# Output pass with seven products in seven of eight token blocks, and all of x turned by TensorE, in place of the second half of x transposed by DMA

## The chip, the cores and the metric

The program runs on one core of one Trainium2 chip. The metric is the device time of one execution in microseconds (us), the median over several runs. Times inside an execution come from the hardware profiler, and are counted from the first instruction. The engines are TensorE (PE; its loads of stationary operands are PEld), VectorE (DVE), ScalarE (ACT), GpSimd (POOL) and SyncE (SP). SP and POOL issue most of the DMA transfers, each from a queue that it works through in order.

## The reference

A gate mixes a spectral filter with a two-layer perceptron, and the program computes the output and eight gradients:

```python
g = sigmoid((x * gate_w).sum(-1, keepdims=True))
a = irfft2(rfft2(x) * (w_r + 1j * w_i))          # spectral filter over (S, D)
h = relu(B_x @ w1 + b1) ** 2                     # inside the vjp as below
b = h @ w2 + b2
out = g * a + (1 - g) * b
# outputs: out, and the gradients of x, w_r, w_i, w1, b1, w2, b2, gate_w for grad_out
```

In the reference the perceptron reads the same `x` as the filter. Here S = 2048 tokens, D = 1024, F = 3584, and inputs and outputs are bf16. In the program, "x" is that input and "grad" is `grad_out`.

## The kernel before, in words

Tokens are cut into 16 tiles of 128 rows, numbered 0 to 15. TensorE carries three large stages one after the other, and the spectral filter is a side generator (`aside`) whose steps `spread` puts between them at a set rate.

**`mlp_in` (0 to about 475 us).** It makes the hidden layer and its gradient, transposed. Its first 32 steps ("units", numbered `u` from 0) work on the first four column blocks of w1 and w2: eight `forth` units (product `ph`, 8 matmuls of 128x512, then on ACT `rT` (relu) and `h2T` (square)), eight `back_` units (product `pd`, 8 matmuls, then one DVE operation into `dhT`) for tokens 0 to 1023; then the same sixteen for tokens 1024 to 2047. A `forth` unit needs four tiles of `xT` (x turned, features on the partitions), a `back_` unit four tiles of `dbT` (the gradient turned). Products take their PSUM banks from a ring of two.

Each tile of x is loaded by SP (`rows_of_x`, tile `xsrc`, eight buffers). `turn_tile` turns a tile: eight 128x128 transposes on TensorE into a PSUM buffer `pt` (a ring of two, tag `tr`), then one copy out of it. Copies into `xT` are mostly ACT's, copies into `dbT` are DVE's. `weigh(i)` is a DVE operation that reads `xsrc` and leaves the gate's sum for the tile (`gsum`). `gate(i0)` takes four such sums, runs two sigmoids on ACT (`omg`, `gcol`) and then four DVE operations that scale the gradient tiles (`dbn`).

In this kernel, x tiles 0 to 7 are turned by TensorE, and tiles 8 to 15 reach `xT` by DMA transposes that SP issues (`turned`), four ahead of the loads of tiles 8 to 11 and four ahead of tiles 12 to 15. `weigh` for a tile after the third is ordered behind the last copy out of a `pt` buffer (`later["copied"]`), and so are `gate`'s scalings. `gate(4)` stands behind unit 6, `gate(8)` behind 15, `gate(12)` behind 19. After unit 17 the first-stage loads (`xs`, tile `src`) and the first `folds` of the filter are put in; `folds` starts with two DVE operations into `uv` and goes on with small ACT copies into `f` (line 263 is the first of them).

All engines execute in order. The order on each engine is fixed when the program is built: a scheduler places the instructions, and `after(..., NoSync)` adds ordering without a wait.

**`mlp_grads` (475 to 837 us).** The gradients of w2 and w1, with seven products in place of eight (sums and differences of quarter matrices, made by DVE).

**`mlp_out` (837 us to the end).** First the output rows. w2's left half (`cL`) is there already; its right half (`cR`, tile `w2R`) is loaded by seven SP transfers of 512 KB. Tokens come in eight blocks of 256 (`load("h", k)`, `even` and `odd` buffers in turn). Here the first two blocks (`N0 = 2`) are done plainly: for each token tile `t` and half `hf` of the columns, 28 matmuls of 128x512 into `acc`, in the order of `steps`. The other six blocks use `Block`, seven chains of 14 matmuls: `p1`, `p2`, `p6`, `p5`, `p7`, `p4`, `p3`. They need four sums of quarters of w2 (`w2_sums`, made by DVE in four steps, names `T1` to `T4`; T3 is written over `cR`) and four sums per block (`sums`, `S1` to `S4`, tiles `dS`). Chain `p6` reads S2 and T2, `p5` reads S1 and T1, `p7` S3 and T3, `p4` T4, `p3` S4. `prepare(t)` (ACT `na`, DVE `v`), `close(t)` (DVE `cu`, a reduction, ACT `scaled`) and `put(t)` finish a token tile. All DVE work of this stage is chained in program order by `dve`, all ACT work by `act`.

The filter's last part (`fft_out`) runs beside it until block 5. For each of its tiles TensorE does `pki` (8 small matmuls, from the ACT copies `re` and the DVE sums `rf`) and `pui` (8 small matmuls); ACT copies `rt` and `e`; DVE does `ev`, `tt`, `yo`. POOL loads `r` and stores `yo`.

Of the kernel before, what the change touches and what calls it, by code (L numbers as in the profile page):

```python
# [10 lines left out]
P = 128  # L11
# [3 lines left out]
ALU = mybir.AluOpType  # L15
# [125 lines left out]
def kernel(  # L141
# [89 lines left out]
    def of_tile(i):  # L231
        return slice(P * i, P * (i + 1))

    def after(ins, earlier, wait=mybir.DependencyClass.Sync):

        if earlier is not None:
            info = mybir.DependencyInfo(wait, mybir.DependencyReason.DATA)
            tc.add_manual_dep(ins.ins, earlier.ins.name, info, reason="paced")
# [375 lines left out]

    def rows_of_w2(t_, fc, half, tie=None):
        src = B_w2[fc * P : (fc + 4) * P, half * H : (half + 1) * H]
        after(ld(out=t_[:, fc : fc + 4, :], in_=src.rearrange("(q p) e -> p q e", p=P)), tie)

    db_p, db_s = pool("db")
    dbn = db_p.tile([P, NT, D], BF16, name="dbn", tag="dbn")  # L620
# [22 lines left out]
    def turn_tile(dst, i, src, copy, tie=None):  # L643

        pt = tps.tile([P, DC, P], BF16, name="pt", tag="tr", bufs=2)
        for b in range(DC):
            later["turned"] = nc.tensor.transpose(pt[:, b, :], src[:, b * P : (b + 1) * P], identb[:])
            after(later["turned"], tie, mybir.DependencyClass.NoSync)
        later["copied"] = copy(out=dst[:, :, of_tile(i)], in_=pt[:])

    def vectors(vrow):
        vps = tps.tile([P, FC], BF16, name="vps", tag="tr", bufs=2)
# [8 lines left out]
        nc.scalar.copy(out=gwb[:], in_=pb[:])  # L661
        return gwb

    def weigh(i, src, tie):
        unused = f1.tile([P, 2, H], FDT, name="uv", tag="uv", bufs=2)
        weighed = nc.vector.tensor_tensor_reduce(
            out=unused[:].rearrange("p a b -> p (a b)"), in0=src[:], in1=gwb[:], scale=1.0, scalar=0.0,
            op0=ALU.mult, op1=ALU.add, accum_out=gsum[:, i : i + 1],
        )
        after(weighed, tie, mybir.DependencyClass.NoSync)  # L670

    def gate(i0):

        c_ = slice(i0, i0 + 4)
        nc.scalar.activation(omg[:, c_], gsum[:, c_], ACT.Sigmoid, scale=-1.0)
        nc.scalar.activation(gcol[:, c_], gsum[:, c_], ACT.Sigmoid)
        for i in range(i0, i0 + 4):
            later["scaled"] = nc.vector.tensor_scalar(out=dbn[:, i, :], in0=dbn[:, i, :], scalar1=omg[:, i : i + 1], scalar2=None, op0=ALU.mult)
            after(later["scaled"], later["copied"], mybir.DependencyClass.NoSync)

    def first_stage_of_x():
        f, ft = {0: folds(f1, xs[0], later["last"])}, {}
# [160 lines left out]
    def mlp_grads():  # L843
# [151 lines left out]
        class Turned(Block):  # L995

            def operands(self):
                (self.a11, self.a12), (_, self.a22) = quads(xr, H)
                (self.b11, self.b21), (_, self.b22) = quads(grp[self.g], FH)
                self.S, self.T = X_, T_.setdefault(self.g, {})  # L1000

            flat = staticmethod(lambda ap: ap.rearrange("p (j f) -> p j f", j=2))

# [3 lines left out]
                return t_  # L1007

            def add(self, t_, h, kept):
                ins = super().add(t_, h, kept)  # L1010
                in_turn(ins, "DVE")
                turn["DVE"] = ins
                return ins

            def side(self, t_, h):
                return t_.rearrange("p (j h f) -> p h j f", j=2, h=2)[:, h]
# [39 lines left out]
        def sums_of_group(g, *which, tie=None):  # L1056
            (g11, g21), (g12, g22) = quads(grp[g], FH)
            made = T_.setdefault(g, {})
            for n in which:
                if n == 3:  # L1060
                    made[3] = fp16(g12)
                else:
                    tag = {1: "S3", 2: "S2", 4: "S4"}[n]
                    made[n] = sb.tile([P, KH, FH], FP16, name=f"G{n}", tag=tag, bufs=2 if n == 1 else 1)[:]
                x, y = {
                    1: lambda: (g12, g11),
                    2: lambda: (g22, made[1]),
                    3: lambda: (g22, g12),
                    4: lambda: (g21, made[2]),
                }[n]()  # L1070
                ins = V(out=made[n], in0=x, in1=y, op=ALU.subtract)
                after(ins, tie, mybir.DependencyClass.NoSync)
                if g > FG:
                    in_turn(ins, "DVE")
                    turn["DVE"] = ins

        NB = 2 * len(jobs)
        each, slow, none = 0.5, 0.25, 1e-6
        for k in range(2):
            blk[k] = Block(k)  # L1080
        fetch(1, 0, 1)
# [85 lines left out]
        fetch(FG + 1, 1)  # L1167
        yield each
        c.p1()
        yield slow  # L1170
        c.p2()
        yield slow
        sums_of_x(3, tie=c.first)
        b.p5()
        sums_of_group(FG, 4, 3)
        fetch(FG + 2, 0)
        yield slow
        b.p6()
        yield slow
        c.p5()  # L1180
        yield slow
        c.p6()
        sums_of_x(4)
        yield each
        b.p7()
        yield each
        c.p7()
        yield each
        b.p4()
        yield each  # L1190
# [3 lines left out]
        for k in range(NB // 2 + 2, NB):  # L1194
            g, second = divmod(k, 2)
            b = Turned(k)
            b.p1()
            if not second:
                sums_of_group(g, 1, 2)
            yield each  # L1200
            b.p2()
            if second:
                fetch(g + 2, 0)
            yield each
            a.p4()
            if not second:
                sums_of_group(g, 3, 4)
            yield each
            b.p6()
            yield each  # L1210
            a.p3()
            if not second:
                fetch(g + 1, 1)
            yield each
            b.p5()
            yield each
            b.p7()
            yield each
            n = k - NB // 2 - 2
            if n < FC // 4:  # L1220
                rows_of_w2(later["w2L"], 4 * n, 0, b.added)
            a = b
# [23 lines left out]
    def mlp_out():  # L1246
# [37 lines left out]

        def fetch_a(t):
            a_[t] = row("a_", FDT)
            ld(out=a_[t][:], in_=ax_scr[0][t][:])

        def fetch_g(t):
            go[t] = row("go3", BF16)  # L1290
            ld(out=go[t][:], in_=go_perm[t])

        def prepare(t):
            na[t], v[t] = row("na"), row("v")
# [165 lines left out]
            right(T4, cL[:, hi], T2)  # L1460

        blks["h", 0] = later["block"]
        N0 = 2
        fetch_a(0), fetch_g(0), fetch_a(1)
        fetch_g(1)
        made = w2_sums()
        load("h", 1, tie=later["tie"])
        for fc in range(0, FC, 4):
            rows_of_w2(cR, fc, 1)
        steps = [(0, 0), (1, 0), (2, 0), (0, 1), (1, 1), (2, 1), (3, 0), (3, 1)]  # L1470
        for t, hf in steps:
            k, t2 = divmod(t, 2)
            acc = mps.tile([P, H], FP32, name="acc", tag=("pX", "pV")[hf], bufs=2)
            for c in range(FC):
                turn["PE"] = mm(acc[:], lhsT=blks["h", k][:, c, t2 * P : (t2 + 1) * P], rhs=(cL, cR)[hf][:, c, :], start=(c == 0), stop=(c == FC - 1))  # L1475
            act(nc.scalar.copy(out=fresh(t)[:, (L, R)[hf]], in_=acc[:]))
            turn["copy"] = turn["ACT"]
            if hf:
                if t:
                    put(t - 1)  # L1480
                if t + 1 < 2 * N0:
                    prepare(t + 1)
                close(t)
                fetch_a(t + 2)
                if t + 2 < 2 * N0:
                    fetch_g(t + 2)
                if t == 1:
                    load("h", 2)
            yield 2.0
            n = steps.index((t, hf))  # L1490
            if n == 2:
                prepare(0)
            if 3 <= n < 5:
                next(made)

        wq = iter(())
# [182 lines left out]
    rows = {}  # L1679
# [7 lines left out]
            queued(ld(out=dbn[:, i, :], in_=go_perm[i]))  # L1687

    def turn_x(i):
        if i >= NT // 2:  # L1690
            weigh(i, rows.pop(i), later["copied"])
            return
        turn_tile(xT, i, rows[i], nc.vector.tensor_copy if i in (1, 3) else nc.scalar.copy, later["gate_row"] if i == 2 else later.get("product"))
        if i >= 3:
            for n in range(4 if i == 3 else 1):
                weigh(n if i == 3 else i, rows.pop(n if i == 3 else i), later["copied"] if i == 3 else None)

    def turn_grad(i):
        turn_tile(dbT, i, dbn[:, i, :], nc.vector.tensor_copy, later["product"])
# [32 lines left out]
    gate(0)  # L1732
    next(units)
    rows_of_grad(1)
    for k in (2, 3):
        for i in range(4 * k, 4 * (k + 1)):
            queued(turned(xT[:, :, of_tile(i)], x_perm[i]))
        rows_of_x(k)
        rows_of_grad(k)
    for t_, n in ((kf, "kf"), (flip, "flip"), (sel, "sel"), (cf, "cf")):  # L1740
        after(st(out=t_[:], in_=cten[n].ap()), later["scaled"])
    stage = None
# [2 lines left out]
    for u in range(32):  # L1745
        for i in before.get(u, ()):
            turn_x(i)
        for i in grads_before.get(u, ()):
            turn_grad(i)
        next(units)  # L1750
        if u in (6, 15, 19):
            gate({6: 4, 15: 8, 19: 12}[u])
        if u == 17:
            for n in range(3):
                xs[n] = source(n, x_perm)
            stage = first_stage_of_x()
        if u > 19 and u % 2:
            next(stage)
# [57 lines left out]
    for _ in spread(grads, spec, rate):  # L1816
        pass
    later["side"] = spec
    early = 8 * 2.0 + 3 * 7
    last_rate = (total - count[0]) / (early - 2.0)  # L1820
    for _ in spread(mlp_out(), spec, last_rate):
        pass
# [33 lines left out]
```

## Time and profile before

| | before |
|---|---|
| time, median of 3 runs (lowest, highest) | 1207.96 us (1206.89, 1208.85) |
| the profiled execution: its time, and the span of its instructions | 1206.89 us, 1205.1 us |
| TensorE busy in that span | 1182.8 us (98%) |
| VectorE, ScalarE, GpSimd busy | 845.4, 614.4, 365.5 us |
| mean granted TensorE clock | 0.998 |
| share of TensorE in the chain that ended last | 88% |

The profiled execution is the fastest of the three runs. The profile's page gives busy time per engine, a chain of work followed back from the last instruction, and groups of instructions by line. A timeline lists instructions of one engine in order of time: start, duration, engine, line, operation, output and inputs, shape, count, and in brackets the idle time ahead of it and what ended it. Matmuls overlap, so a matmul's own duration (379 ns for 128x512) is longer than the step from one to the next (8 of them take 1.73 us, 0.216 us each).

### The profile page before, as it was taken

The numbers are of one execution on the slowest core, as the hardware profiler recorded it, in microseconds if no ns is written. First come the engines' busy times: TensorE is split into PE (matmuls) and PEld (weight loads), VectorE is DVE, ScalarE is ACT, GpSimd is POOL, SyncE is SP. The second block draws the span as 40 slices with busy tenths as digits, with TensorE's granted clock in tenths as the row PEclk, the third lists the DMA queues.
The fourth block names the chain that finished last, engine by engine and source line by source line (L and its number), as shares of the span: only waits on it lengthen the run. The fifth ranks groups of instructions, "written<-read, shape, count | busy, mean of one in ns | idle before, by whom it ended". The sixth has DMA issues, their size and how long they took to land.

```text
span 1205.1 us, 19779 instructions
## 1 busy us (share of the span) xinstructions
PE 1182.8 (98%) x7055; PEld 647.7 (54%) x7149; DVE 845.4 (70%) x1842; ACT 614.4 (51%) x1121; POOL 365.5 (30%) x587
## 2 busy tenths in 40 slices
PE   9899999999999999999999999999999999999998
PEld 5455545544444444444447888888544544444444
DVE  5766546676878887877789846665489866966464
ACT  6257757755777863444444425554455523232322
POOL 1024434413455451433333353545132100000000
PEclk9999999999999999999999999999999999999999
DMA  9957576686757598999999799976976699965551
GB/s 273 288 160 206 137 203 191 165 166 183 208 171 208 180 231 169 188 202 226 226 189 188 179 214 200 209 202 197 283 212 178 195 206 249 246 203 173 158 152 35
DMA packets 341104, 236.53 MB, mean 196 GB/s; under 512 B 206237, under 2 KB 299963, under 8 KB 341004
## 3 DMA queue, kind: packets, MB, share of 16 engines
q1 hardware_dynamic: 309552, 144.08, 54.0%
q0 software_dynamic: 30224, 90.61, 24.8%
q8 instruction: 56, 0.92, 0.3%
q10 hardware_dynamic: 1228, 0.57, 0.2%
q14 instruction: 44, 0.36, 0.1%
HBM read 107.24 MB, written 81.81 MB: 157 GB/s over the span
## 4 chain that ended last, share of the span: by engine, by line
PE 88%; DVE 4%; DMA 4%; ACT 2%; issue 1%; POOL 0%; SPq 0%; ACTq 0%; DVEq 0%
PE pd L755 15%; PE ph L747 15%; PE pX L1378 13%; PE pV L1378 10%; PE pX L947 8%; PE pX L1023 6%; PE pV L947 6%; PE pV L1023 5%; PE acc L1475 2%; PE pu L310 2%; PE pk L277 1%; PE px L416 1%; DMA xsrc<-in_A_x_dram 1%; DMA r<-y_scr 1%; PE pv L447 1%
## 5 line engine op out<-in xcount | busy, mean ns | idle before, releaser
L747 PE MATMUL ph<-xT,w1g 128*128 128x512 bf16 x867 | 216.0, 381 | 7.3 <-ACT rT L748 4.5
L755 PE MATMUL pd<-dbT,w2T 128*128 128x512 bf16 x876 | 209.5, 379 | 0.9
L755 PEld LDWEIGHTS <-w2T 128*128 128x128 bf16 x896 | 87.1, 98 | 102.9
L747 PEld LDWEIGHTS <-w1g 128*128 128x128 bf16 x896 | 85.6, 98 | 99.1 <-issue 6.5
L759 DVE SCALAR_TENSOR_TENSOR dhT<-pd,rT 128x512 bf16<-128x512 f32 x108 | 74.3, 688 | 77.8 <-PE pd L755 62.8
L748 ACT ACTIVATE rT<-ph,b1col 128x512 bf16<-128x512 f32 x108 | 74.5, 690 | 49.1 <-PE ph L747 46.3
L1023 PEld LDWEIGHTS <-res 128*128 128x128 bf16 (+1 forms) x896 | 86.7, 98 | 11.7 <-issue 0.8
L1378 PEld LDWEIGHTS <-dS 128*128 128x128 f16 x588 | 57.2, 98 | 66.0 <-issue 0.7
L226 POOL DMA_DIRECT2D r<-y_scr x96 | 58.4, 613 | 102.7 <-ACT re L553 56.0
L419 ACT CAST x<-px 64x512 f16<-64x512 f32 x128 | 74.2, 580 | 27.1 <-PE px L416 26.0
L226 POOL DMA_DIRECT2D z_scr<-u x96 | 58.6, 617 | 92.0 <-ACT u L294 48.0
L1023 PEld LDWEIGHTS <-X 128*128 128x128 f16 x672 | 64.9, 98 | 7.9
L749 ACT ACTIVATE h2T<-rT 128x512 bf16<-128x512 bf16 x108 | 67.9, 628 | 2.3
L1378 PEld LDWEIGHTS <-odd 128*128 128x128 bf16 (+1 forms) x392 | 38.2, 98 | 45.3
L1378 PEld LDWEIGHTS <-even 128*128 128x128 bf16 (+1 forms) x392 | 38.0, 98 | 44.3
L456 POOL DMA_DIRECT2D y_scr<-pc x64 | 36.1, 565 | 63.1 <-DVE pc L453 60.3
L947 PEld LDWEIGHTS <-S 128*128 128x128 f16 x336 | 32.8, 98 | 39.7 <-DVE S L921 0.3
L394 POOL COPY w<-wn 128x512 bf16<-128x512 bf16 x32 | 24.3, 760 | 90.7 <-DVE tt L427 73.4
L1400 DVE TENSOR_TENSOR cu<-pV,u 128x512 f16<-128x512 f32 x27 | 18.6, 690 | 40.9 <-PE pV L1378 34.8
L1351 POOL DMA_DIRECT2D out_dram<-gxo x14 | 7.6, 540 | 130.8 <-DVE gxo L1350 130.8
L1378 PE MATMUL pX<-wT,dS 128*128 128x512 f16 x196 | 44.6, 379 | 0.0
L810 POOL DMA_DIRECT2D h2T_scr<-h2T x28 | 20.7, 740 | 75.5 <-ACT h2T L749 42.0
(275 smaller groups left out, 2471.4 us busy)
## 6 DMA issues: line engine op xcount, KB each, us to landing
h2T_scr<-h2T POOLq DMA_DIRECT2D x28, 512.0 KB, 4.2
dhT_scr<-dhT POOLq DMA_DIRECT2D x28, 512.0 KB, 5.9
z<-z_scr SPq DMA_DIRECT2D x64, 128.0 KB, 3.2
y_scr<-pc POOLq DMA_DIRECT2D x64, 128.0 KB, 4.0
ax_scr<-yo POOLq DMA_DIRECT2D x32, 256.0 KB, 5.3
out_dram<-whi POOLq DMA_DIRECT2D x28, 256.0 KB, 5.6
out_dram<-wlo POOLq DMA_DIRECT2D x28, 256.0 KB, 5.3
even<-h2T_scr SPq DMA_DIRECT2D x8, 896.0 KB, 6.2
```

What stands on the lines that cost most here:

```text
L226: issue(out=a, in_=b) if stored else issue(out=b, in_=a)
L394: G.tensor_copy(out=w[:, 0:2, 0:HW].rearrange("p c (g i) -> p c g i", g=4), in_=wn[:, :, h * HW : (h + 1) * HW].rearrange("p c (i g) -> p ...
L419: nc.scalar.copy(out=x[lanes[n], c, :, 0:HW], in_=px[lanes[c], n])
L456: st(out=y_scr[:][c, :, :, h].rearrange("r x t l -> (r x) t l"), in_=pc[:, n])
L747: opened(mm(ph[:], lhsT=w1g[:, dc, fc % 2 * P : (fc % 2 + 1) * P], rhs=xT[:, dc, ss], start=(dc == 0), stop=(dc == DC - 1)), fc)
L748: nc.scalar.activation(rT[:], ph[:], ACT.Relu, bias=b1col[:, fc : fc + 1])
L749: nc.scalar.activation(h2T, rT[:], ACT.Square)
L755: opened(mm(pd[:], lhsT=w_[:, ec, fc % FGC * P : (fc % FGC + 1) * P], rhs=dbT[:, ec, ss], start=(ec == 0), stop=(ec == DC - 1),), fc)
L759: return STT(out=dhT, in0=pd[:], scalar=2.0, in1=rT[:], op0=ALU.mult, op1=ALU.mult, accum_out=gb1part[:, fc, sb : sb + 1],)
L947: self.mm = mm(acc[:], lhsT=lhs[:, t, c_], rhs=rhs[:, t, :], start=start and t == 0, stop=t == KH - 1, skip_group_check=True,)
L1023: ins = mm(acc[:, j * FH : (j + 1) * FH], lhsT=lhs[:, t, c_], rhs=rhs[:, t, :], start=start and first_ is None, stop=t == KH - 1, skip_gro ...
L1378: pe(mm(acc[:], lhsT=lhs[:, c, :], rhs=rhs[:, c, :], start=start and c == 0, stop=c == KH - 1, skip_group_check=True,))
```

## The change

x tiles 8 to 15 are turned by TensorE as tiles 0 to 7 are, at units 12 to 19, and the eight DMA transposes go. `weigh` runs beside each turning and is ordered behind an early copy alone; the orderings behind `later["copied"]` go, and `gate(4)` moves from unit 6 to unit 3. In `mlp_out` only the first block is plain (`N0 = 1`), so four half tiles stand ahead of the blocks with seven products instead of eight. The seven loads of w2's right half go ahead of the small loads and of block 1. The first two steps of `w2_sums` follow half tiles 3 and 4 instead of 4 and 5. In `mlp_grads` the DVE sums for a group of w1 columns are put at the end of the block before, some DVE orderings go, and the side work is spread evenly over five steps that had a smaller weight.

```diff
     def turn_tile(dst, i, src, copy, tie=None):
...
-        later["copied"] = copy(out=dst[:, :, of_tile(i)], in_=pt[:])
+        copy(out=dst[:, :, of_tile(i)], in_=pt[:])
...
-        after(weighed, tie, mybir.DependencyClass.NoSync)
+        after(weighed, later.get("b1"), mybir.DependencyClass.NoSync)
...
             later["scaled"] = nc.vector.tensor_scalar(out=dbn[:, i, :], in0=dbn[:, i, :], scalar1=omg[:, i : i + 1], scalar2=None, op0=ALU.mult)
-            after(later["scaled"], later["copied"], mybir.DependencyClass.NoSync)
...
-        each, slow, none = 0.5, 0.25, 1e-6
+        each, none = 0.5, 1e-6
...
         c.p7()
+        sums_of_group(FG + 1, 1, 2, tie=c.added)
...
             b.p1()
-            if not second:
-                sums_of_group(g, 1, 2)
...
             b.p7()
+            if second and g + 1 < len(jobs):
+                sums_of_group(g + 1, 1, 2, tie=b.added)
...
-        N0 = 2
-        fetch_a(0), fetch_g(0), fetch_a(1)
-        fetch_g(1)
+        N0 = 1
         made = w2_sums()
-        load("h", 1, tie=later["tie"])
         for fc in range(0, FC, 4):
-            rows_of_w2(cR, fc, 1)
-        steps = [(0, 0), (1, 0), (2, 0), (0, 1), (1, 1), (2, 1), (3, 0), (3, 1)]
+            loaded = rows_of_w2(cR, fc, 1)
+        for ins in (fetch_a(0), fetch_g(0), fetch_a(1), fetch_g(1)):
+            after(ins, loaded, mybir.DependencyClass.NoSync)
+        steps = [(0, 0), (1, 0), (0, 1), (1, 1)]
...
-                if t == 1:
-                    load("h", 2)
             yield 2.0
             n = steps.index((t, hf))
-            if n == 2:
+            if n == 0:
+                load("h", 1, tie=turn["PE"])
+            if n == 1:
                 prepare(0)
-            if 3 <= n < 5:
+            if n >= 2:
                 next(made)
...
     def turn_x(i):
-        if i >= NT // 2:
-            weigh(i, rows.pop(i), later["copied"])
-            return
-        turn_tile(xT, i, rows[i], nc.vector.tensor_copy if i in (1, 3) else nc.scalar.copy, later["gate_row"] if i == 2 else later.get("product"))
-        if i >= 3:
-            for n in range(4 if i == 3 else 1):
-                weigh(n if i == 3 else i, rows.pop(n if i == 3 else i), later["copied"] if i == 3 else None)
+        src = rows.pop(i)
+        weigh(i, src)
+        turn_tile(xT, i, src, nc.vector.tensor_copy if i == 1 else nc.scalar.copy, later["gate_row"] if i == 2 else later.get("product"))
...
-    for k in (2, 3):
-        for i in range(4 * k, 4 * (k + 1)):
-            queued(turned(xT[:, :, of_tile(i)], x_perm[i]))
-        rows_of_x(k)
-        rows_of_grad(k)
+    rows_of_x(2)
+    rows_of_grad(2)
+    rows_of_x(3)
+    rows_of_grad(3)
...
-        if u in (6, 15, 19):
-            gate({6: 4, 15: 8, 19: 12}[u])
+        if u in (3, 15, 19):
+            gate({3: 4, 15: 8, 19: 12}[u])
...
-    early = 8 * 2.0 + 3 * 7
+    early = 4 * 2.0 + 4 * 7
```

More of the change, by code (lines that the diff above doesn't have):

```diff
@@ L616, in rows_of_w2 @@
         src = B_w2[fc * P : (fc + 4) * P, half * H : (half + 1) * H]
-        after(ld(out=t_[:, fc : fc + 4, :], in_=src.rearrange("(q p) e -> p q e", p=P)), tie)
+        loaded = ld(out=t_[:, fc : fc + 4, :], in_=src.rearrange("(q p) e -> p q e", p=P))
+        after(loaded, tie)
+        return loaded
     db_p, db_s = pool("db")
@@ L662, in everywhere, with weigh @@
         return gwb
-    def weigh(i, src, tie):
+    def weigh(i, src):
         unused = f1.tile([P, 2, H], FDT, name="uv", tag="uv", bufs=2)
@@ L999, in operands @@
                 (self.b11, self.b21), (_, self.b22) = quads(grp[self.g], FH)
-                self.S, self.T = X_, T_.setdefault(self.g, {})
+                self.S, self.T = X_, T_[self.g]
             flat = staticmethod(lambda ap: ap.rearrange("p (j f) -> p j f", j=2))
@@ L1009, in add @@
             def add(self, t_, h, kept):
[L1010 to L1013, printed above, removed]
+                turn["DVE"] = super().add(t_, h, kept)
+                return turn["DVE"]
             def side(self, t_, h):
@@ L1070, in sums_of_group @@
                 }[n]()
[L1071 to L1075, printed above, removed]
+                after(V(out=made[n], in0=x, in1=y, op=ALU.subtract), tie, mybir.DependencyClass.NoSync)
         NB = 2 * len(jobs)
-        each, slow, none = 0.5, 0.25, 1e-6
+        each, none = 0.5, 1e-6
         for k in range(2):
@@ L1169, in mlp_grads @@
         c.p1()
-        yield slow
+        yield each
         c.p2()
-        yield slow
+        yield each
         sums_of_x(3, tie=c.first)
@@ L1176, in mlp_grads @@
         fetch(FG + 2, 0)
-        yield slow
+        yield each
         b.p6()
-        yield slow
+        yield each
         c.p5()
-        yield slow
+        yield each
         c.p6()
@@ L1286, in fetch_a @@
             a_[t] = row("a_", FDT)
-            ld(out=a_[t][:], in_=ax_scr[0][t][:])
+            return ld(out=a_[t][:], in_=ax_scr[0][t][:])
         def fetch_g(t):
             go[t] = row("go3", BF16)
-            ld(out=go[t][:], in_=go_perm[t])
+            return ld(out=go[t][:], in_=go_perm[t])
         def prepare(t):
```

## The prediction

> **What bounds the kernel now.** I read the page first: engines, then groups.
>
> ```profile
> PE 1182.8 (98%) x7055; PEld 647.7 (54%) x7149; DVE 845.4 (70%) x1842; ACT 614.4 (51%) x1121; POOL 365.5 (30%) x587
> ```
>
> TensorE is the bound, so a change can win only by fewer TensorE steps or fewer of its waits. By steps this change is nearly neutral: 14 matmuls of 128x512 go (112 of a plain block become 7 x 14), 64 transposes come. What decides are waits. The TensorE timeline shows one at the start of `mlp_in`; the windows (columns: PE, PEld, DVE, ACT, POOL busy, clock, DMA share, GB/s) give its clock.
>
> ```profile
> 52.17 0.61 PE L647 MATMUL pt<-identb,dbn 128*128 128x128 bf16 x8
> 57.33 3.57 PE L747 MATMUL ph<-xT,w1g 128*128 128x512 bf16 x8 [4.55 <-ACT rT L748]
> ```
> ```profile
> 52.70:57.30 4.60, 0.08 (x2) 0.00 (x0) 2.42 (x7) 1.60 (x5) 0.00 (x0) 1.00 1.18 295
> 57.30:61.00 3.70, 3.67 (x13) 1.42 (x13) 3.70 (x11) 2.22 (x6) 0.00 (x0) 0.54 1.08 228
> ```
>
> An idle 4.55 us, and then eight matmuls in 3.57 us where eight others (27.94, below) take 1.89, at a granted clock of 0.54. The hole is worth 4.55 + 1.70 = 6.25 us. Its cause is in the timelines of ACT and of SP's queue (start, time to issue).
>
> ```profile
> 56.50 0.20 ACT L263 COPY f<-uv 128x2 f16<-128x2 f16 x1 [2.13 <-DVE uv L257]
> 56.60 0.68 ACT L748 ACTIVATE rT<-ph,b1col 128x512 bf16<-128x512 f32 x1
> ```
> ```profile
> 19.03 2.01 SPq L1687 DMA_DIRECT2D dbn<-in_grad_out_dram  x4
> 21.08 7.85 SPq L181 DMA_TRANSPOSE xT<-in_A_x_dram  x4
> 29.06 2.07 SPq L637 DMA_DIRECT2D xsrc<-in_A_x_dram  x4
> 34.06 8.50 SPq L181 DMA_TRANSPOSE xT<-in_A_x_dram  x4
> 42.67 2.64 SPq L637 DMA_DIRECT2D xsrc<-in_A_x_dram  x4
> 48.73 1.66 SPq L637 DMA_DIRECT2D src<-in_A_x_dram  x3
> ```
>
> ACT's `f` waits for `uv`, which waits for `src`, issued at 48.73; `rT`, which frees TensorE's bank, stands behind `f`. The eight transposes hold SP's queue for 7.85 + 8.50 = 16.35 us ahead of `src`.
>
> In the output pass (t counts from 837.56, its start) TensorE waits four times between 877 and 903 us, 1.16 + 0.27 + 0.23 + 0.30 = 1.96 us, mostly for `re` and `rf`, whose work is queued behind DVE's sums of w2:
>
> ```profile
> 870.92 3.88 DVE L1442 TENSOR_TENSOR wT<-w2R,w2L 128x7168 f16<-128x7168 bf16 x1
> 879.23 3.89 DVE L1442 TENSOR_TENSOR wT<-w2R,wT 128x7168 f16<-128x7168 bf16 x1
> ```
> ```profile
> 901.56 2.75 PE L1378 MATMUL pX<-wT,dS 128*128 128x512 f16 x12
> ```
>
> T1 runs at t = 33.4 and T2 ends at 45.5, while `p6`, the first to need T2, starts at 64.0: 18 us in hand.
>
> **Start of `mlp_in`.** (a) Eight tiles turned by TensorE: 0.445 us each (the step of tiles 0 to 7 in the timeline), **+3.56**. (b) The transposes go: `src` is issued about 16 us earlier, near 33, and lands near 40, before its readers. The hole goes, **-6.25**. The eight copies that come to ACT fit: in units 16 to 19 a copy of 0.9 beside `rT` and `h2T` (0.59 + 0.53) makes 2.03 us of a unit's 2.17.
>
> (c) A new wait. In the instruction order of the built program DVE no longer finishes its `dbT` copies ahead of the weighing. Before, it runs `dbT` 0 to 2, then scales the gradient tiles 4 to 7, then `dbT` 3 and 4. After: `dbT` 0, scale 4 to 7, weigh 8, `dbT` 1, weigh 9, `dbT` 2, weigh 10, weigh 11, `dbT` 3. Here are these copies before, on DVE, and the transposes that wait for their buffers, on PE:
>
> ```profile
> 21.62 0.69 DVE L649 COPY dbT<-pt 128x1024 bf16<-128x1024 bf16 x1 [0.72 <-PE pt L647]
> 23.79 0.69 DVE L649 COPY dbT<-pt 128x1024 bf16<-128x1024 bf16 x1 [1.48 <-PE pt L647]
> 24.40 1.66 DVE L678 TENSOR_SCALAR dbn<-dbn,omg 128x1024 bf16<-128x1024 bf16 x4
> 25.98 0.68 DVE L649 COPY dbT<-pt 128x1024 bf16<-128x1024 bf16 x1
> ```
> ```profile
> 27.49 0.61 PE L647 MATMUL pt<-identb,dbn 128*128 128x128 bf16 x8
> 27.94 1.89 PE L755 MATMUL pd<-dbT,w2T 128*128 128x512 bf16 x8
> ```
>
> Gradient tiles 4 to 7 are issued at 19.03 to 20.6 and land 4.3 to 4.5 us later: scaling ends at about 25.7. The load of x tile 8, right behind them, lands at about 26.0 (25.3 to 26.3 by the queue's 0.67 us per transfer). A weighing has a pitch of 1.15 us (row of 1.22), a copy one of 0.60. So weigh 8 ends at 27.15, `dbT` 1 at 27.75 (TensorE's fourth gradient turn waits for its buffer, due at 25.32: 2.4 us idle), weigh 9, `dbT` 2 at 29.5, weigh 10 and 11, `dbT` 3 at 32.4. The first `pd` needs that and starts at 32.45 in place of 27.94 or so: **+4.4**, and about 0.2 more as the same DVE work repeats behind unit 15: **+4.6**. Bounds: 3 if tile 8 lands as the gradients do and weighings overlap, 6.5 if the loads that now follow without pause land later by 2 us. Sum for the start: 3.56 - 6.25 + 4.6 = **+1.9** (0.3 to 3.8).
>
> **`mlp_grads`.** Sums made a block earlier and side steps spread evenly: TensorE waits 0.3 to 0.7 us in 100 here and DVE has room between the sums. Nothing, within 1 us; without that room a sum of some 1 us would stand in front of its chain.
>
> **Output pass.** (a) 14 matmuls less at 0.216: **-3.02**. (b) The four waits belong to the old order: **-1.96**. (c) The half of w2 is issued at t = 0 in place of 4.7. Seven transfers landed a median of 11.0 us after issue before; I estimate all landed by 15 to 17, and acc(0,1) needs the first at 13.6 and the last at 18.8. Nothing taken; up to 3.5 if the small loads, now issued behind it, and it share the queues badly. (d) The DVE chain. After acc(1,1) (t = 26.65) TensorE has only `p1` and `p2` (3.02 each) and filter steps before `p6`, due at t = 33.9. DVE does in program order: `v`, `cu`, a reduction and a filter group once ACT's `na(1)` has come at 21.2 (0.61 + 0.72 + 1.15 + 0.19 + 2.36), so T1 starts at 26.3 (3.80); then `ot`, `cu`, a reduction and its tail (0.6 + 0.72 + 1.34), T2 from 32.7 to 36.5; then S3, S1, S2 for `p6` (1.12 + 1.12 + 1.01):
>
> ```profile
> 867.22 1.22 DVE L1308 CUSTOM_DVE_ANT_0 ot<-cu,go 128x1024 bf16<-128x1024 f16 x1
> 868.56 0.28 DVE L582 TENSOR_TENSOR ev<-e 128x256 f16<-128x256 f16 x1
> ```
> ```profile
> 895.59 1.08 DVE L1374 TENSOR_TENSOR dS<-even 128x1792 f16<-128x1792 bf16 x1
> ```
>
> S2 ends at 39.8, `p6` waits 5.9 us. `p6` itself, `p5` and `p7` take 9 us, but DVE goes on being late: `ot` and a group's part (1.3) ahead of `rf`, T3 and T4 (7.6), two `v` and a `cu` (1.8), the sums of block 2 (3.25). From T1's start that is 35.0 us of DVE work, so it ends at 61.3, and the `rf` and sums that TensorE would want at 51.5 come then: **+9.8** in all, 5.9 of it at `p6`. Bounds 6 (only `p6`) and 12 (T1 2 us later, by the row of `na`). Sum: -3.02 - 1.96 + 9.8 = **+4.8** (1 to 7; 10.5 with w2 late).
>
> Row and rule: the hole above cost 1.70 us in clock after 4.55 us idle. [...] I take no clock loss in the sum, because DVE, not TensorE, sets the time behind `p6`; 1.7 is kept as the upper bound.
>
> Total: +1.9 + 4.8 = +6.7 on the profiled execution's 1206.89, so 1213.6; the median of the runs lies 1.07 above that execution, half of which goes on top: **1214**.
>
> **Rivals.** *The sums come in time* (the other side): S2 done by t = 33.9, so `p6` doesn't wait. Then -5.0 + 1.9 = -3.1: 1203.8. It decides when T1 starts 5.9 us earlier, at 20.4; for it, DVE is 70% busy and some filter work could slide; against it, T1 stands behind `v` of tile 1 in the order, and that needs a half tile which ends at 19.65. Chance 0.10. *The start costs nothing*: x tile 8 lands by 21.4 in place of 26.0. Then -2.7 + 4.8 = +2.1: about 1209. Against it, it is queued behind gradients that land at 23.3 at the earliest. Chance 0.10. *More is late*: w2's half late by up to 3.5 us and the clock's 1.7: 1216 to 1219. Chance 0.15. *The hole stays* (the change doesn't do what it says): ACT waits for the gate of tiles 12 to 15 in place of `src`, and up to 6 are not won: 1218 to 1220; the weighing of tile 12 now has its load at about 30, so 0.05.
>
> **How the numbers follow.** My own case has 0.60, 1210 to 1216. From 1207 to 1219 the range leaves out most of the faster case and the last end of the late ones. About 0.2% (2.4 us) is what a measurement can tell from no change: below 1205.5 lies the faster rival with a little of the second, 0.10; within it the rest of the second and the low end of mine, 0.12; above it 0.78.
>
> **What would show it.** Right: no TensorE idle near 53 and full clock at 57; the first `pd` near 32, with its `dbT` copies between weighings; T1 at t = 26 and an idle of 5 to 6 us ahead of `p6`, released by DVE's `dS`; later waits for `rf`. Wrong: `pd` at 28 (no wait at the start), `p6` near t = 34, TensorE waits on w2's half, or a gap in `mlp_grads`.

## The result, and the profile after

| | before | after |
|---|---|---|
| median of 4 runs (lowest, highest) | 1207.67 us (1206.89, 1208.85) | 1217.76 us (1216.02, 1220.02) |
| ratio to before | | 1.0084, 95% interval 1.0064 to 1.0104 |
| the profiled execution: time, span | 1206.89, 1205.1 us | 1220.02, 1218.2 us |

The change makes the kernel 10.1 us slower; 6.0 were forecast, in the same direction. The profiled execution of after is the slowest of its four, that of before the fastest, so the two traces differ by 13.1 us. (Of the experiments below, the last has a wide interval: five of its executions took 1199.9 to 1201.0 us and four 1205.0 to 1209.4, and no run shows why.) Two marks in the TensorE timeline cut the span into stages: the last `pd`, and the first `acc` of the output pass.

| profiled execution | start to last `pd` | last `pd` to first `acc` (nearly all `mlp_grads`) | first `acc` to the end |
|---|---|---|---|
| before | 461.5 | 376.1 | 367.5 |
| after | 465.9 (+4.4) | 381.3 (+5.2) | 371.0 (+3.5) |
| forecast | +1.9 | 0 | +4.8 |

The page's engine line shows that little of it is work. TensorE's busy time is up by 4.7 us, part of which is the same matmuls at half the clock; the span is up by 13.1.

```profile
PE 1187.5 (97%) x7104; PEld 652.2 (54%) x7199; DVE 851.2 (70%) x1848; ACT 624.1 (51%) x1130; POOL 364.6 (30%) x587
```

**The start.** SP's queue, then TensorE's timeline:

```profile
33.13 1.63 SPq L639 DMA_DIRECT2D src<-in_A_x_dram  x3
```
```profile
28.10 0.61 PE L649 MATMUL pt<-identb,dbn 128*128 128x128 bf16 x8 [2.49 <-DVE dbT L651]
...
32.83 3.21 PE L756 MATMUL pd<-dbT,w2T 128*128 128x512 bf16 x8 [1.95 <-DVE dbT L651]
...
56.23 1.89 PE L748 MATMUL ph<-xT,w1g 128*128 128x512 bf16 x8
```

`src` is issued at 33.13 in place of 48.73, the hole near 53 is gone, and at 56 TensorE runs at full speed. The new wait is where the built order put it: idle 2.49 and 1.95 us (2.4 and about 2.0 worked out beforehand), the first `pd` at 32.83 (32.45). What was not forecast is its 3.21 us: the clock halved behind the second gap (granted 0.50 from 33.20 to 36.60). DVE's timeline has what stands ahead of the copies (0.08 us reads of an accumulator are left out):

```profile
23.46 1.09 DVE L680 TENSOR_SCALAR dbn<-dbn,omg 128x1024 bf16<-128x1024 bf16 x2 [2.44 <-DMA dbn<-in_grad_out_dram]
...
25.42 0.65 DVE L680 TENSOR_SCALAR dbn<-dbn,omg 128x1024 bf16<-128x1024 bf16 x1 [0.19 <-DMA dbn<-in_grad_out_dram]
26.21 1.22 DVE L668 CUSTOM_DVE_ANT_0 uv<-xsrc,gwb 128x1024 f16<-128x1024 bf16 x1
27.36 0.69 DVE L651 COPY dbT<-pt 128x1024 bf16<-128x1024 bf16 x1
27.96 1.22 DVE L668 CUSTOM_DVE_ANT_0 uv<-xsrc,gwb 128x1024 f16<-128x1024 bf16 x1
29.10 0.69 DVE L651 COPY dbT<-pt 128x1024 bf16<-128x1024 bf16 x1
29.71 1.21 DVE L668 CUSTOM_DVE_ANT_0 uv<-xsrc,gwb 128x1024 f16<-128x1024 bf16 x1
30.85 1.22 DVE L668 CUSTOM_DVE_ANT_0 uv<-xsrc,gwb 128x1024 f16<-128x1024 bf16 x1
31.99 0.69 DVE L651 COPY dbT<-pt 128x1024 bf16<-128x1024 bf16 x1
```

The scalings wait for gradient tiles, the weighings come behind them, and the copy that the first `pd` needs starts at 31.99.

**`mlp_grads`.** Here before had no such wait: `wlo` ran ahead of the sums `G`, and TensorE's chain came without idle (TensorE, then DVE):

```profile
665.92 1.91 PE L1023 MATMUL pV<-even,res 128*128 128x256 bf16 x16
```
```profile
665.19 0.68 DVE L958 TENSOR_TENSOR wlo<-pV,u 128x512 bf16<-128x512 f32 x1
665.79 1.21 DVE L1071 TENSOR_TENSOR G<-even 128x2048 f16<-128x2048 bf16 x1
```

TensorE after, and DVE:

```profile
667.57 1.91 PE L1022 MATMUL pV<-odd,X 128*128 128x256 bf16 x16 [0.65 <-DVE whi L959]
...
673.64 2.37 PE L1022 MATMUL pV<-even,res 128*128 128x256 bf16 x16 [1.99 <-DVE wlo L959]
675.81 3.15 PE L1022 MATMUL pX<-G,res 128*128 128x256 f16 x16
```
```profile
668.83 1.22 DVE L1070 TENSOR_TENSOR G<-even 128x2048 f16<-128x2048 bf16 x1
...
670.30 1.22 DVE L1070 TENSOR_TENSOR G<-even,G 128x2048 f16<-128x2048 bf16 x1
...
671.76 1.22 DVE L1070 TENSOR_TENSOR even<-even 128x2048 f16<-128x2048 bf16 x1
672.90 0.69 DVE L959 TENSOR_TENSOR wlo<-pV,u 128x512 bf16<-128x512 f32 x1
```

`wlo` is the copy that frees a PSUM bank. Three sums of w1's next group, moved ahead by the change, now stand in front of it, and TensorE waits 1.99 us. Two chains behind it take 2.37 + 3.15 us where such a row takes 1.91 otherwise: half clock again (granted 0.50 from 674.90 to 678.30), 1.66 us by their starts (673.64 to 678.80 in place of two steps of 1.75).

**The output pass** (t counts from 847.20). DVE, then TensorE:

```profile
873.60 3.88 DVE L1438 TENSOR_TENSOR wT<-w2R,w2L 128x7168 f16<-128x7168 bf16 x1
...
880.10 3.89 DVE L1438 TENSOR_TENSOR wT<-w2R,wT 128x7168 f16<-128x7168 bf16 x1
...
886.15 1.09 DVE L1370 TENSOR_TENSOR dS<-odd 128x1792 f16<-128x1792 f16 x1
```
```profile
881.98 0.40 PE L566 MATMUL pki<-ki,re 128*128 128x128 f16 x4 [1.01 <-ACT re L553]
887.30 1.46 PE L1374 MATMUL pX<-wT,dS 128*128 128x512 f16 x3 [4.93 <-DVE dS L1370]
```

T1 starts at t = 26.4 (26.3 worked out), S2 ends at 40.0 (39.8), and TensorE waits 1.01 us for `re` and 4.93 us at `p6` itself, 5.94 in all (5.9). Then the clock is halved until about 893 (granted 0.50 from 886.50 to 893.30).

### The profile page after: what moved, and what is told of

The parts are those of the page before. It is cut to its first block, busy times and chain, and to the rows that moved or that the text cites. A ratio compares the mean times of both kernels' runs of the same rounds, so it can differ in the third digit from the quotient of the medians.

```text
span 1218.2 us, 19882 instructions
## 1 busy us (share of the span) xinstructions
PE 1187.5 (97%) x7104; PEld 652.2 (54%) x7199; DVE 851.2 (70%) x1848; ACT 624.1 (51%) x1130; POOL 364.6 (30%) x587
## 5 line engine op out<-in xcount | busy, mean ns | idle before, releaser
L1374 PEld LDWEIGHTS <-dS 128*128 128x128 f16 x630 | 61.7, 99 | 77.0 <-DVE dS L1370 5.1
L1374 PEld LDWEIGHTS <-odd 128*128 128x128 bf16 (+1 forms) x448 | 43.4, 98 | 50.8
L1374 PE MATMUL pX<-wT,dS 128*128 128x512 f16 x210 | 50.7, 394 | 4.9 <-DVE dS L1370 4.9
L568 ACT CAST rt<-pki 128x1024 f16<-128x1024 f32 x32 | 32.4, 1012 | 30.9 <-PE pki L566 30.7
```

Source lines behind the costliest of these rows:

```text
L568: nc.scalar.copy(out=rt[n][:], in_=pk[:])
L1374: pe(mm(acc[:], lhsT=lhs[:, c, :], rhs=rhs[:, c, :], start=start and c == 0, stop=c == KH - 1, skip_group_check=True,))
```

## The experiments

Each kernel ran in 5 rounds beside the kernel before; the ratio is to that. Stage lengths are those of each kernel's profiled execution.

**Grads as before.** All edits of `mlp_grads` undone.

> The kernel after, with all edits of mlp_grads undone (the sums of w1's groups back at the head of their own block, the DVE orderings and the smaller weights back). Theory (three separate losses; this one is DVE's: sums moved together with side work stand ahead of the copies that free TensorE's banks): the waits of 0.65 and 1.99 us near 668 to 674 and the half-clock stretch behind them (1.7 us) go, 4.3 to 5.2 us less than the kernel after: about 1213, ratio to before 1.0045. Rival (the stall is a matter of when the side work falls after the longer start, not of these edits): the two waits stay, about 1217.8, ratio 1.008.

Measured: 1216.14 us, ratio 1.0069 (1.0055 to 1.0082). `mlp_grads` takes 375.9 us, as before, and both waits are gone: the theory holds for the stage. But the output pass grew from 371.0 to 375.2, which neither theory had, so the total gained only 1.6.

**Weighing later.** The start's DVE order alone:

```diff
-        weigh(i, src)
+        weigh(i, src, later["copied"] if i >= NT // 2 else None)
...
+            after(later["scaled"], later["copied"], mybir.DependencyClass.NoSync)
...
-            gate({3: 4, 15: 8, 19: 12}[u])
+            gate({6: 4, 15: 8, 19: 12}[u])
```

> The kernel after, with only DVE's order at the start changed: weighing of tiles 8 to 15 ordered behind the last copy out of a transpose buffer, the scalings too, gate(4) back behind unit 6. The eight tiles are still turned by TensorE. Theory (the start's wait is DVE's order): first pd at 28 in place of 32.8, no half clock behind it, 6.0 to 6.5 us less than the kernel after: about 1211.5, ratio 1.003; the start then is 2.7 us shorter than before's (3.56 for the turns, 6.25 for the hole). Rival (eight more turns and copies don't fit into units 12 to 19, so that gates and ACT's copies take the wait's place): at most 2 us less, about 1216, ratio 1.007.

Measured: 1212.29 us, ratio 1.0030 (1.0019 to 1.0041), 5.5 less than after where 6.0 to 6.5 were expected. No TensorE idle over 0.6 us is left from 20 to 60 us. (The first `pd` is at 30.53 in this trace: here the wait for the first loads, 1.98 us ahead of the first product, was longer than in before (1.02), and half clock followed it: eight matmuls at 13.91 took 2.65 us, eight at 16.84 took 1.89.) The turns themselves fit; the order of DVE was the loss. This run moves weighings, scalings and `gate(4)` together; a run below parts them.

**Sums first.** The same work in the output pass in another DVE order:

```diff
+            if (t, hf) == steps[-1]:
+                first = Block("h", N0)
+                first.sums(3, 1, 2)
             if hf:
-                if t:
-                    put(t - 1)
                 if t + 1 < 2 * N0:
                     prepare(t + 1)
-                close(t)
+                    close(t)
...
-            if n == 1:
-                prepare(0)
-            if n >= 2:
-                next(made)
+            if n in (1, 2):
+                next(made)
+            if n == 1:
+                prepare(0)
...
             b.p6()
             if a is not None:
                 put(2 * k - 1)
+            else:
+                put(2 * k - 2)
+                close(2 * k - 1)
```

> The kernel after, with DVE's order at the start of the output pass changed: T1 behind half tile 2, T2 behind half tile 3 and directly followed by S3, S1, S2 of block 1; the closing of token tile 1 and its stores behind p6. Same work. Theory (p6 waits for DVE's chain T1, T2, S2, which is queued behind the closing of tiles): S2 ends near t = 34 of the pass in place of 40, the wait of 4.9 us ahead of p6 and the half clock behind it (1.7 us) go, some 3 us come back in block 2, where DVE is still late: 4 to 5 us less than the kernel after, about 1213.3, ratio 1.0045. Rival (the same 35 us of DVE work sets the time wherever it lies, and filter steps behind T1 make TensorE wait for rf): at most 1 us less, 1217, ratio 1.0075.

Measured: 1209.81 us, ratio 1.0016 (1.0008 to 1.0024): 8 us less than after, more than the theory had. DVE and TensorE (t counts from 843.66):

```profile
853.94 3.89 DVE L1438 TENSOR_TENSOR wT<-w2R,w2L 128x7168 f16<-128x7168 bf16 x1 [0.45 <-DMA w2R<-in_B_w_dram]
```
```profile
878.00 0.23 PE L566 MATMUL pki<-ki,rf 128*128 128x128 f16 x1 [0.34 <-DVE rf L558]
878.87 0.34 PE L566 MATMUL pki<-ki,rf 128*128 128x128 f16 x3 [0.64 <-DVE rf L559]
879.05 3.19 PE L1374 MATMUL pX<-wT,dS 128*128 128x512 f16 x14
```

T1 starts at t = 10.3, because it needs only the first half of the loads, and 16 us earlier than in after. `p6` waits for nothing, the waits of the pass up to t = 60 sum to 1.6 us, all for `rf` and `re`, and the clock stays at full speed. The pass takes 363.2 us. The rival, that 35 us of DVE work set the time wherever they lie, falls: DVE had idle time ahead of T1 to put them into (in after four waits, 14.4 us in all, between 847 and 873).

**All three together.**

> The three of them together: the kernel after with mlp_grads as before, with the weighing later and with the output pass's sums first. Theory (three separate losses that add up): 1217.8 less 4.7, 6.2 and 4.5, about 1202.4, ratio 0.9955, faster than before. Rival (the losses overlap, since a stage that starts earlier meets the same DMA and DVE due times): 1207 or more, ratio 1.000 or more.

Measured: 1204.24 us, ratio 0.9967 (0.9955 to 0.9979), 1.8 above the theory. Start 459.0, `mlp_grads` 375.9, output pass 367.6: the first two add up, the pass is again 4 us longer with `mlp_grads` as before.

**Slow weights, and sums back.** These two split the edits of `mlp_grads`: one puts back only the five smaller weights (`yield slow` for `yield each`), the other only the sums' old place and the DVE orderings.

> The kernel after with only the five smaller weights of the side work in mlp_grads back (sums of w1's groups stay early). First run of this study showed that undoing all edits of mlp_grads shortens that stage by 5.4 us and lengthens the output pass by 4.2. Theory (the two come from one edit: even spreading pulls a step of the filter out of the output pass into mlp_grads, where its DVE work meets the early sums): the waits near 668 to 674 go here too, the output pass is about 375 us in place of 371: about 1216.5, ratio 1.007. Rival (the early sums alone make the stage's waits, the output pass's loss comes from the sums' absence): the waits stay, 1217.8 or more.

> The kernel after with the sums of w1's groups back in their own block and DVE's orderings back, the side work still spread evenly. In the built program three sums of 1.2 us no longer stand ahead of the copy wlo that TensorE waited 1.99 us for; the copy whi (0.65 us) stands where it did. Theory (moved sums cost the 1.99 us, and at times the half clock behind it; even spreading costs the 0.65 and gives back 4.2 in the output pass): mlp_grads about 376.5 to 377.5, output pass 371: 1213 to 1214, ratio 1.005. Rival (even spreading makes both waits): no change, 1217.8.

Measured: slow weights 1217.40 us, ratio 1.0088 (1.0075 to 1.0101); sums back 1212.88 us, ratio 1.0049 (1.0037 to 1.0061).

| profiled execution | sums early | sums as before |
|---|---|---|
| even weights: `mlp_grads`, output pass | 381.3, 371.0 (after) | 376.8, 369.6 (sums back) |
| smaller weights: `mlp_grads`, output pass | 377.9, 374.6 (slow weights) | 375.9, 375.2 (grads as before) |

The early sums cost `mlp_grads` 2.0 to 4.5 us (1.7 of the larger figure is half clock). Even weights cost it 0.9 with the sums as before, and give 3.6 to 5.6 back in the output pass. For the sums-back run the theory's numbers came within 1.4 us, except that a wait for a sum `G` (1.33 us) took the place of that at `wlo`. For the slow-weights run the theory was half wrong: a wait of 1.77 us for `wlo` stays with the smaller weights.

Why the pass is longer with the smaller weights: counted by their rows, one more filter step's `pki` (8 small matmuls, 0.44 us) is left for it, and the wait at `p6` is longer, 6.94 us in place of 1.01 + 4.93, as is the half clock behind it. How much of the difference is the extra step and how much its place on DVE, the runs don't separate. Part of it may not be due to the weights at all; the run with the pass alone, below, bears on this.

```profile
885.34 6.02 PE L1374 MATMUL pX<-wT,dS 128*128 128x512 f16 x14 [6.94 <-DVE dS L1370]
```

This line is `p6` in the slow-weights run: 14 matmuls in 6.02 us, which take 3.19 in the sums-first run.

**All even.** Weighing later, sums first, sums of w1's groups back, even weights kept.

> The version that should beat both: weighing later, output pass's sums first, sums of w1's groups back, side work spread evenly. It is the combined kernel of before (1204.2) with the output pass of the sums-first run (363.2 us in place of 367.6) and 0.65 us more in mlp_grads. Theory (stages add up): 1200 to 1201, ratio 0.994. Rival (the 4 us in the output pass came from the time at which it starts, not from the filter step that is left over): 1204, ratio 0.997.

Measured: 1201.80 us, ratio 0.9958 (0.9946 to 0.9970): 0.8 above the theory. The stages nearly add up (459.3, 376.8, 363.9), and it beats both kernels.

**Turns alone.** The kernel before with the start alone changed.

> The kernel before with the start alone changed: all of x turned by TensorE, no DMA transposes, DVE's weighing behind the last copy out of a transpose buffer as before. Theory (the turns cost 3.56 us, the hole of 6.25 goes, nothing takes its place): 2.7 us less, about 1205, ratio 0.9978. Rival (what the start gains is lost later, because later due times of DMA and filter set the end): 1207.7, ratio 1.000.

Measured: 1204.89 us, ratio 0.9983 (0.9974 to 0.9992), 2.4 less than before. Its trace is of a slower execution (1206.79): the start ends at 459.4, 2.1 earlier than in before, but the output pass takes 369.7, 2.2 more (4.3 us of waits against 2.5). So +3.56 - 6.25 stands by the median and by the stage; in that one execution the gain was lost again later, as the rival has it.

**Weighing tied, scalings free.**

> The kernel after with only the weighing of tiles 8 to 15 ordered behind the last copy; the scalings stay free and gate(4) stays at unit 3. In the built program the scalings of tiles 4 to 7 then stand behind dbT 0 and ahead of dbT 1 to 4, with no weighing between. Theory (each DVE operation ahead of a copy counts): the scalings end near 25.7, TensorE's fourth gradient turn waits about 1 us in place of 2.5, the first pd starts near 29 in place of 32.8, mostly without the half clock: 4.5 to 5.5 us less than the kernel after, 1212.5 to 1213.5, ratio 1.0045. Rival (the position of the scalings, waiting for the gradient tiles to land, is what delays, and the weighings only follow): the first pd at 31 or later, at most 2 us less, ratio 1.007.

Measured: 1212.36 us, ratio 1.0042 (1.0030 to 1.0054). TensorE:

```profile
26.86 0.61 PE L649 MATMUL pt<-identb,dbn 128*128 128x128 bf16 x8 [0.75 <-DVE dbT L651]
...
29.48 1.89 PE L756 MATMUL pd<-dbT,w2T 128*128 128x512 bf16 x8
```

The scalings, waiting for gradient tiles, cost 0.75 us; the weighings behind them cost the rest of the start's loss. The rival falls.

**The pass alone.** The kernel before with the output pass alone changed.

> The kernel before with the output pass alone changed (one plain block, w2's half first, its sums two half tiles earlier; start and mlp_grads as before). Theory (p6's wait for DVE is the pass's own, and with the smaller weights one more filter step meets it): output pass about 375 us in place of 367.5, about 1215, ratio 1.006. Rival (the longer pass was a matter of the changed start or of the even spreading): 1207.7 less 5 for the fewer products and the waits that go, 1203, ratio 0.996.

Measured: 1212.46 us, ratio 1.0059 (1.0035 to 1.0082), a pass of 372.0 us. `p6` waits 6.93 us there too:

```profile
879.16 5.16 PE L1380 MATMUL pX<-wT,dS 128*128 128x512 f16 x14 [6.93 <-DVE dS L1376]
```

So the pass loses by itself, without the changed start; the size is below the 375 expected. The grads-as-before run has the same `mlp_grads` and the same pass, and its pass took 375.2: there `p6`'s 14 matmuls took 6.04 us, here 5.16, and a wait of 0.44 us for a load and one of 0.64 for `re` stand against one of 0.18 for `re` here, together 1.8 of the 3.2 us. Between these two kernels only the start differs, so some 3 us of a pass can come with the start or with the execution, and part of the 3.6 to 5.6 us above may not be the weights'.

**One sum early.** All even, with the first of the two sums (`sums_of_group(FG + 1, 1, tie=c.added)`) early.

> The fastest kernel so far (1201.8) with one of the two moved sums of the first turned group of w1 put early again, between two copies out of PSUM. There TensorE still waits 1.33 us for the second sum, near 670. Theory (one sum of 1.2 us fits into DVE's slack ahead of wlo, which was 3.7 less 1.99 us; three did not): the wait of 1.33 falls to 0.3 or less and none comes at wlo: about 1200.7, ratio 0.995. Rival (any sum ahead of wlo makes TensorE wait there): 1201.8 or more.

Measured: 1201.02 us, ratio 0.9968 (0.9949 to 0.9988): by time, the two fastest versions can't be told apart. In the trace the wait of 1.33 us is gone and `wlo` makes none, as the theory has it; `mlp_grads` takes 375.8 us in place of 376.8.

## Why the prediction was right, and where it was wrong

- **The start's hole, -6.25, and the turns, +3.56: right.** With the DVE order mended they stand alone and give -2.4 in place of -2.7 (-2.1 by the stage).
- **The start's new wait, +4.6: right in kind, place and length of the idle (2.49 + 1.95), too small in cost.** The step that failed is one not written down: no clock loss was counted for these two gaps. In the window from 32.80 to 36.70 the granted clock was 0.56, worth about 1.7 us. The other 0.8 between +1.9 and the measured +4.4 come mostly from two small waits outside the argument: 0.55 us more ahead of the first product, a wait that ranges from 1.02 to 1.98 us in the traces, and 0.47 for a load near 441. The stage grew above the stated 3.8.
- **`mlp_grads`, nothing within 1 us: wrong, +5.2.** The step "DVE has room between the sums" asked when the sums are needed, and not what is queued behind them. DVE had the room, but the copies that free TensorE's banks stand in the same queue. The stage's waits sum to 4.35 us against 1.49 before; with 1.66 of half clock and 0.44 for the filter step that moved here that makes 5.0 of the 5.2.
- **The output pass, +4.8: right in place and mechanism, 1.3 too high.** T1, S2 and the 5.94 us of waits up to `p6` came within 0.3 us of the working; 1.01 of them were for `re`, as 1.16 of before's four waits were, so `p6` itself waited 4.93. The rest of the 9.8 took another form: not later waits for `rf` and sums (0.16 us measured), but half clock. From `p6`'s start (887.30) to the next step (893.74) pass 6.44 us, where its matmuls and an `rf` group would need some 3.4 with the short wait: 3.0 lost, where the prediction's upper bound had 1.7. So 6.1 + 3.0 = 9.1. The argument that a clock loss would not add, because DVE sets the time behind `p6`, fits the trace: from T1 to the `rf` of the next block, at t = 60.9 (DVE's work was to end at 61.3), DVE idled 0.74 us, and TensorE came for that `rf` without a wait. One sum of the prediction can't be followed: the terms listed for DVE's 35.0 us add up to 27.5. In the trace the same stretch, T1 to block 2's S2, takes 34.1 us, because filter groups of 2.37 us, which the list leaves out, stand in it. The filter step that moved out (-0.44) had not been counted.
- **The rivals.** "The sums come in time" did not occur in after, and occurs in the sums-first run: the pass takes 363.2 us there, 4.3 less than before, where the forecast had -5.0. "The start costs nothing" did not occur. "More is late" half occurred: w2's half was in time, but the clock was lost. The median lies in that rival's 1216 to 1219, above the 1210 to 1216 of the prediction's own case.
- **The sum.** +1.9, 0 and +4.8 against +4.4, +5.2 and +3.5 in a pair of executions that lie 3 us further apart than the medians. The direction follows from the mechanism; that the range held the median is partly luck. Its upper end had been set by late loads and the clock, and of these only the clock came; the early sums in `mlp_grads`, the stage that grew most, were in no term.

## What to carry to other kernels

Work moved to an engine "with room" is priced at what stands behind it in that engine's queue: look for the copies that free the bound engine's banks, in the built order, not at the engine's busy share. A transfer that goes away gives its full gain only if the order of the work that hung on it is kept. And price a new idle of TensorE like those here twice, with and without half clock behind it: the 1.99 us ahead of a chain of `mlp_grads` cost 1.66 more in after and nothing more in the weighing-later run, and behind the 4.93 us at `p6` in after 3.0 were lost.

## What the runs showed of the hardware

Half clock also followed idle gaps much shorter than the 4.55 us of before, and not every time. The same 1.99 us gap at the same instruction was followed by 2.37 and 3.15 us for two groups of sixteen matmuls in after, and by 1.91 us in the sums-first run and in the weighing-later run:

```profile
669.02 1.91 PE L1023 MATMUL pV<-even,res 128*128 128x256 bf16 x16 [1.99 <-DVE wlo L960]
```

At the start it followed the gap of 1.95 us in after, and none of the gaps (2.33, 1.94) in the slow-weights run. Behind the waits of 4.92 to 6.94 us at `p6` it came in each of the seven traces that had them; in after TensorE was busy for 5.84 us of the 886.50 to 893.30 that were granted 0.50. A drop cost 1.70 us in before and 1.66 in `mlp_grads` of after, and the times of after range over 4.0, so by the author's estimate such drops can be some of the spread from run to run. What decides whether a gap of about 2 us is followed by half clock, these runs do not show.
